# Last 128 rows of w1 on 64 partitions, and a reshaped tail, in a decode step of attention and SwiGLU

## Chip, cores, metric

One core of one Trainium2 chip. Time is device microseconds (us) of one execution; medians of several executions are quoted. Runs 1 to 4 were on one chip, runs 5 to 11 on another.

## The reference, cut to what matters

```python
x = A_x                                  # [4, 1, 640], bf16
xn = layernorm(x)
# attention: 32 heads of 192, the last 2048 positions of the cache (8192 long), wq [640, 6144], wo [6144, 640]
# SwiGLU: h = silu(xn @ w1) * (xn @ w3);  h @ w2,  w1 and w3 [640, 1536], w2 [1536, 640]
return x + attention(xn, k_cache, v_cache, wq, wo) + swiglu(xn, w1, w3, w2)
```

Four tokens read 223 MB of cache and weights (222.97 MB on q1 in the page of the kernel before). Nothing is used twice, so the DMA is the work.

## The kernel before

All loads are issued on one queue (SyncE). K and V of a head are 3 MB each, one row of 24,576 bytes per partition. w1 and w3 are loaded in one transfer each, five rows of 3,072 bytes per partition. The queue ends with the last two V, the first eight chunks of w2, two pieces of wo, and two pieces of w2 of two chunks each.

```python
def load_v(h):
    vt = vpool.tile([P, NJ, Dh], BF16, tag="vt")
    nc.sync.dma_start(out=vt[:].rearrange("q j d -> q (j d)"),
                      in_=v_win[:, h].rearrange("b (p j) d -> p b (j d)", p=PB))
    vts[h] = vt
# ... cut ...
def ffn_load(name, w):
    wt = fpool.tile([P, KC, F], BF16, tag="w", name=name)          # P = 128, KC = 5, F = 1536
    nc.sync.dma_start(out=wt[:].rearrange("p k n -> p (k n)"), in_=w.rearrange("(p kc) n -> p (kc n)", kc=KC))
    ffn[name] = wt

def ffn_in(name):                                                   # xn @ w1 or xn @ w3
    ffn["ps"] = ps_t.tile([P, FW], FP32, tag="t", name="f_ps")
    for kc in range(KC):
        for w in range(HG):
            nc.tensor.matmul(ffn["ps"][w * CT:(w + 1) * CT, :], lhsT=xnT[:, kc].rearrange("p a b -> p (a b)")[:, 0:CT],
                             rhs=ffn[name][:, kc, w * FW:(w + 1) * FW], start=(kc == 0), stop=(kc == KC - 1))
# ... cut ...
W2C = [0, FC - 4, FC - 2, FC]                                       # FC = 12 chunks of w2
# ... cut: the schedule; its end loads V 30 and 31, w2 piece 0, wo 6 and 7, w2 pieces 1 and 2 ...
nc.vector.tensor_copy(out=res[:, 0:N0 // 2], in_=acc[0:NR, 0:N0 // 2])
nc.scalar.copy(out=res[:, N0 // 2:N0], in_=acc[0:NR, N0 // 2:N0])
```

## Time and profile before

| | before |
|---|---|
| time, median of 3 | 527.62 us |
| span of the profile | 525.5 us |
| DMA queue q1, share of 16 engines | 98.9% |
| PE, DVE busy | 67%, 66% |
| last landing of w2 | 521.79 us |

From the page of the kernel before: the busy tenths of the DMA in 40 slices, and the DMA queues (packets, megabytes, share of the time of 16 engines); the line of q10, 16 packets in 0.01 MB, is left out here and below.

```profile
DMA  8999999999999999999999999999999999999995
...
q1 hardware_dynamic: 11536, 222.97, 98.9%
q8 instruction: 15, 0.25, 0.2%
q14 instruction: 5, 0.04, 0.0%
```

The DMA is full nearly from start to end: 9 tenths in every slice but the first and the last. Two small queues share its engines: 15 packets of 16,384 bytes and 5 of 8,192 bytes inside the span, both of kind "instruction"; this document calls them fetches.

The chain of waits of the kernel before, from 514 us on (start, duration, what):

```profile
490.75 31.04 DMA w<-in_B_w_dram
521.79 0.04 issue
521.83 0.45 PE acc L214 x4
522.28 0.02 issue
522.31 0.33 DVE res L442
522.63 0.02 issue
522.66 0.28 ACT res L443
```

The end waits for the last w2 piece; then come four matmuls and two copies, one after the other (both read and write the same tiles; `--waits` has the second, on ACT, released by the first, on DVE), and the output.

In the traces a load over 128 partitions raises its semaphore (the counter that others wait for) 16 times, and at most 16 data packets are under way at once (overlaps of a few ns aside). The packets have no engine numbers; each of the 16 times is read here as the landing on one engine. Here are those of the last w2 piece, sorted (us):

```
518.55 518.61 518.71 518.81 518.96 519.29 519.48 520.00 | 521.44 521.47 521.58 521.60 521.64 521.69 521.69 521.79
```

Eight engines are done about 2 us before the other eight, though all carry the same bytes of q1. The packet records tell why. A data packet of 24,576 bytes takes 912 ns, and an engine starts the next one 908 ns after the last, all the way. Where a q8 packet falls on an engine, it takes 0.88 to 0.96 us itself and the data packet after it takes 1.37 to 1.46 us in place of 0.91: about 1.4 us lost on that engine. A q14 packet takes 0.31 us itself; the data packet after it took 1.44 us in three cases of five, so about 0.85 us was lost, and 1.15 and 1.19 us in the other two.

The q8 packets, all of 16,384 bytes, come one every 26 to 39 us. By the end, engines with equal bytes of q1 are up to 3.2 us apart (518.55 and 521.79 us).

### The profile page before, as it was taken

What the parts mean: (1) busy time and instruction counts of PE and PEld (TensorE: products, weight loads), DVE (VectorE), ACT (ScalarE), POOL (GpSimd) and SP (SyncE); (2) the same over time, 40 slices, a digit from 0 to 9 for tenths busy, and PEclk for the clock granted to TensorE, in tenths of its full rate; (3) what the DMA queues carried; (4) which work ended last, traced back from release to release, by engine and by line L of the source; (5) the groups of instructions that cost most, each with busy time, mean ns of one, the idle gap of its engine ahead of it and who ended that gap; (6) DMA issues with size and microseconds to landing.
All of it is one profiled execution on the core that took longest, in us unless ns stands there. A gap on an engine that the chain in (4) does not pass through costs nothing.

```text
span 525.5 us, 4734 instructions
## 1 busy us (share of the span) xinstructions
PE 354.6 (67%) x2307; PEld 74.0 (14%) x1613; DVE 345.2 (66%) x435; ACT 45.9 (9%) x144; POOL 1.1 (0%) x8
## 2 busy tenths in 40 slices
PE   2765766567747687667748866686685776675685
PEld 0000111111101111011111211111111111111122
DVE  3179755479557767587656776577667766677671
ACT  2111201000000001000000000000000000000001
POOL 0000000000000000000000000000000000000000
PEclk9989978979889979798887998789878998889988
DMA  8999999999999999999999999999999999999995
GB/s 360 430 438 425 440 431 424 436 428 439 425 433 431 435 426 432 434 427 439 430 427 440 425 434 430 436 428 435 432 428 434 430 430 436 430 434 430 434 422 240
DMA packets 11572, 223.26 MB, mean 425 GB/s; under 512 B 1296, under 2 KB 1312, under 8 KB 2592
## 3 DMA queue, kind: packets, MB, share of 16 engines
q1 hardware_dynamic: 11536, 222.97, 98.9%
q8 instruction: 15, 0.25, 0.2%
q14 instruction: 5, 0.04, 0.0%
q10 hardware_dynamic: 16, 0.01, 0.0%
HBM read 222.96 MB, written 0.01 MB: 424 GB/s over the span
## 4 chain that ended last, share of the span: by engine, by line
DMA 66%; PE 17%; DVE 14%; ACT 2%; issue 1%; SPq 0%
DMA kt<-in_A_k_cache_dram 52%; PE ps L244 10%; DVE pr L233 10%; DMA w<-in_B_w_dram 6%; DMA vt<-in_A_v_cache_dram 5%; PE po L317 4%; DMA wt<-in_A_wq_dram 4%; DVE sc L252 2%; PE qps L193 1%; ACT ex L280 1%; DVE z L288 1%; PE mt L274 1%; PE mt L261 0%; ACT negm L277 0%; DVE qbc L199 0%
## 5 line engine op out<-in xcount | busy, mean ns | idle before, releaser
L244 PE MATMUL ps<-pr,idb 128*128 128x512 bf16 x768 | 211.5, 417 | 151.0 <-DVE pr L233 151.0
L233 DVE TENSOR_TENSOR pr<-kt,qbc 128x3072 bf16<-128x3072 bf16 x128 | 223.5, 1747 | 113.8 <-DMA kt<-in_A_k_cache_dram 113.8
L252 DVE TENSOR_REDUCE sc<-ps 128x16 f32<-128x512 f32 x128 | 87.2, 681 | 2.1 <-PE ps L244 2.1
L296 PE MATMUL o_ps<-vt,z 128*8 128x384 bf16 x1024 | 57.4, 365 | 0.2 <-DVE z L288 0.2
L317 PE MATMUL po<-o_sb,sel_w 128*32 128x192 f32 x128 | 49.2, 518 | 0.6 <-ACT o_sb L299 0.6
L296 PEld LDWEIGHTS <-z 128*8 128x8 bf16 x1024 | 25.5, 92 | 91.7 <-issue 81.2
L299 ACT COPY o_sb<-o_ps 128x384 f32<-128x384 f32 x32 | 15.3, 478 | 190.1 <-PE o_ps L296 190.1
L288 DVE TENSOR_TENSOR z<-ex,mask_b 128x256 bf16<-128x256 bf16 x32 | 13.6, 424 | 23.4 <-ACT ex L280 23.4
L277 ACT COPY negm<-mt 128x1 f32<-128x1 f32 x32 | 5.1, 159 | 256.1 <-PE mt L274 256.1
L261 PEld LDWEIGHTS mt<-idf,lmax 128*1 128x1 f32 x32 | 3.2, 100 | 140.8 <-issue 140.8
L193 PE MATMUL qps<-wt,xnT 128*128 128x512 bf16 x60 | 16.1, 428 | 5.1 <-DMA wt<-in_A_wq_dram 5.1
L317 PEld LDWEIGHTS po<-o_sb,sel_w 128*32 128x32 f32 x128 | 13.8, 130 | 29.7 <-issue 28.2
L244 PEld LDWEIGHTS <-idb 128*128 128x128 bf16 x124 | 11.9, 96 | 39.1 <-issue 32.6
L274 PEld LDWEIGHTS mt<-ones_ff,gneg 1*128 1x128 f32 x64 | 9.4, 183 | 46.3 <-issue 20.9
L199 DVE CAST qbc<-qps 128x512 bf16<-128x512 f32 x6 | 3.8, 685 | 18.0 <-PE qps L193 18.0
L274 PE MATMUL mt<-ones_ff,gneg 1*128 1x1 f32 x64 | 12.1, 256 | 0.6 <-DVE gneg L269 0.6
L266 DVE TENSOR_REDUCE gmax<-mt 1x4 f32<-1x128 f32 x32 | 8.8, 274 | 5.4 <-PE mt L261 5.4
L304 PEld LDWEIGHTS po<-rsum,tot_w 128*32 128x32 f32 x64 | 4.4, 108 | 55.6 <-issue 30.6
L280 ACT ACTIVATE ex<-sc,negm 128x64 bf16<-128x64 f32 x32 | 11.1, 348 | 1.0
L261 PE MATMUL mt<-idf,lmax 128*1 128x128 f32 x32 | 11.0, 344 | 0.0
L214 PE MATMUL acc<-wo_t,oT 128*4 128x320 bf16 x96 | 9.2, 298 | 0.6 <-DMA wo_t<-in_A_wo_dram 0.6
L304 PE MATMUL po<-rsum,tot_w 128*32 128x1 f32 x64 | 7.1, 181 | 1.3 <-ACT ex L280 1.3
(53 smaller groups left out, 62.7 us busy)
## 6 DMA issues: line engine op xcount, KB each, us to landing
kt<-in_A_k_cache_dram SPq DMA_DIRECT2D x32, 3072.0 KB, 18.8
vt<-in_A_v_cache_dram SPq DMA_DIRECT2D x32, 3072.0 KB, 25.9
wo_t<-in_A_wo_dram SPq DMA_DIRECT2D x8, 960.0 KB, 21.5
wt<-in_A_wq_dram SPq DMA_DIRECT2D x2, 3072.0 KB, 9.8
w<-in_B_w_dram SPq DMA_DIRECT2D x2, 1920.0 KB, 21.5
wt<-in_A_wq_dram SPq DMA_DIRECT2D x1, 1536.0 KB
w<-in_B_w_dram SPq DMA_DIRECT2D x1, 1280.0 KB, 32.8
w<-in_B_w_dram SPq DMA_DIRECT2D x2, 320.0 KB, 31.0
```

What stands on the lines that cost most here:

```text
L193: nc.tensor.matmul(qp[:], lhsT=xnT[:, kc].rearrange("p a b -> p (a b)"), rhs=wq_rows[kc][:, (c0 + i) * QC:(c0 + i + 1) * QC], start=(kc == ...
L233: nc.vector.tensor_tensor(out=pr[:], in0=kts[h][:, g * JQ:(g + 1) * JQ, :], in1=qbc[:, h * Dh:(h + 1) * Dh].unsqueeze(1).to_broadcast([P, ...
L244: nc.tensor.matmul(ps[:], lhsT=idb[:], rhs=pr[:, :, kk * DD:(kk + 1) * DD], start=(kk == 0), stop=(kk == NK - 1))
L252: nc.vector.tensor_reduce(out=scs[h][:, g * JQ:(g + 1) * JQ], in_=pss.pop(u)[:], axis=AX.X, op=ALU.add)
L261: nc.tensor.transpose(out=mt[0:1, 0:P], in_=chs[h][0][:], identity=idf[:])
L274: nc.tensor.matmul(mt[:, P:P + 1], lhsT=gneg[:].rearrange("o p b -> o (p b)"), rhs=ones_ff[0:1, 0:1], start=True, stop=True)
L280: nc.scalar.activation(out=ex[:], in_=scs.pop(h)[:], func=ACTF.Exp, bias=negm[:, 0:1], scale=SCALE, accum_out=rsum[:])
L288: nc.vector.tensor_tensor(out=z[:], in0=ex[:].unsqueeze(2).to_broadcast([P, NJ, B]), in1=mask_b[:].unsqueeze(1).to_broadcast([P, NJ, B]), ...
L296: nc.tensor.matmul(o_ps[c * CT:c * CT + 2 * B, :], lhsT=z[:, 2 * jj:2 * jj + 2, :], rhs=vt[:, 2 * jj:2 * jj + 2, :], start=(jj < 4), stop= ...
L299: nc.scalar.copy(out=o_sb[:], in_=o_ps[:])
L304: nc.tensor.matmul(po[sl, Dh:Dh + 1], lhsT=tot_w[:].rearrange("p a b -> p (a b)"), rhs=rsums.pop(h)[:], start=True, stop=True)
L317: nc.tensor.matmul(po[sl, 0:Dh], lhsT=sel_w[:, par].rearrange("p a b -> p (a b)"), rhs=o_sb[:, par * Dh:(par + 1) * Dh].rearrange("p (r i) ...
```

## The change

The intent, as it can be read: take load off late engines by loading the last fifth of w1 in two transfers that eight engines carry and that fill partitions 0-63, and shorten the tail: a last w2 piece of one chunk, one copy of the result. w3, w2 and the last V are cut into more transfers. The room comes from the second copy of x and a smaller tile of ones. The core of the diff:

```diff
-    def load_v(h):
+    def load_v(h, n=1):
         vt = vpool.tile([P, NJ, Dh], BF16, tag="vt")
-        nc.sync.dma_start(...)
+        for j in range(0, NJ, NJ // n):
+            nc.sync.dma_start(out=vt[:, j:j + NJ // n]..., in_=...)
@@ cut: x_load and its tile x_res go, x_add uses x_sb; ones_ff [P, P] -> [1, 1] @@
+    LP = P // 2
+    LE, LI = 8, 4
+    LX = (KC - 1) * P
@@ cut: ffn_x, which transposes xn for the new order of rows @@
     def ffn_load(name, w):                       # now for w3 alone
-        nc.sync.dma_start(out=wt[:].rearrange("p k n -> p (k n)"), in_=w.rearrange("(p kc) n -> p (kc n)", kc=KC))
+        for k0, k1 in ((0, KC // 2), (KC // 2, KC)):
+            nc.sync.dma_start(out=wt[:, k0:k1, :]..., in_=...)
+    def ffn_load_low(name, w):
+        wt = fpool.tile([P, KC + 1, F], BF16, tag="w", name=name)
+        nc.sync.dma_start(out=wt[:, 0:KC - 1, :].rearrange("p k n -> p (k n)"),
+                          in_=w[0:LX, :].rearrange("(p kc) n -> p (kc n)", kc=KC - 1))
+        for g in range(2):
+            rows_g = w[LX + g * LP:LX + (g + 1) * LP, :]
+            nc.sync.dma_start(out=wt[g * CT:(g + 1) * CT, KC - 1:KC + 1, :].rearrange("p k n -> p (k n)"),
+                              in_=rows_g.rearrange("(i e j) n -> e i (j n)", i=LI, e=LE))
@@ cut: ffn_in takes a list of (lhsT, partitions); ffn_in_low uses four chunks of 128 rows and two of 64 @@
-    W2C = [0, FC - 4, FC - 2, FC]
+    W2C = [0, FC - 8, FC - 4, FC - 1, FC]
-    add(3, 0, ffn_load, "w1", B_w1)
-    add(11, 7, ffn_in, "w1")
+    add(3, 0, ffn_load_low, "w1", B_w1)
+    add(6, 7, ffn_x)
+    add(11, 7, ffn_in_low, "w1")
@@ cut: the end now loads V 30, V 31 in two halves, w2 pieces 0 and 1, wo 6 and 7, w2 pieces 2 and 3 @@
-    nc.vector.tensor_copy(out=res[:, 0:N0 // 2], in_=acc[0:NR, 0:N0 // 2])
-    nc.scalar.copy(out=res[:, N0 // 2:N0], in_=acc[0:NR, N0 // 2:N0])
+    nc.vector.tensor_copy(out=res[:], in_=acc[0:NR, :])
```

The order `e i` with e = 8 in the source of the small transfers is deliberate.

More of the change, by code (lines that the diff above doesn't have):

```diff
@@ L111, in load_k @@
         kts[h] = kt
-    def load_v(h):
+    def load_v(h, n=1):
         vt = vpool.tile([P, NJ, Dh], BF16, tag="vt")
-        nc.sync.dma_start(out=vt[:].rearrange("q j d -> q (j d)"),
-                          in_=v_win[:, h].rearrange("b (p j) d -> p b (j d)", p=PB))
+        for j in range(0, NJ, NJ // n):
+            nc.sync.dma_start(out=vt[:, j:j + NJ // n].rearrange("q j d -> q (j d)"),
+                              in_=v_win[:, h].rearrange("b (p j) d -> p b j d", p=PB)[:, :, j:j + NJ // n].rearrange("p b j d -> p b (j d)"))
         vts[h] = vt
@@ L140 @@
     make_identity(nc, idf[:])
-    ones_ff = const.tile([P, P], FP32, name="ones_ff")
+    ones_ff = const.tile([1, 1], FP32, name="ones_ff")
     nc.vector.memset(ones_ff[:], 1.0)
@@ L220 @@
     po = ps_po.tile([P, Dh + 1], FP32, name="po")
-    xr = {}
-    def x_load():
-        xr["t"] = const.tile([B, D], BF16, name="x_res")
-        nc.sync.dma_start(out=xr["t"][:], in_=A_x.rearrange("b s d -> (b s) d"))
     def x_add(i):
-        acc_half(i, idb[0:B, 0:B], xr["t"], first=True)
+        acc_half(i, idb[0:B, 0:B], x_sb, first=True)
     def mult(u):
@@ L273, in chain_bc @@
         lmax, mt, gneg = chs[h]
-        nc.tensor.matmul(mt[:, P:P + 1], lhsT=gneg[:].rearrange("o p b -> o (p b)"), rhs=ones_ff[0:1, 0:1],
+        nc.tensor.matmul(mt[:, P:P + 1], lhsT=gneg[:].rearrange("o p b -> o (p b)"), rhs=ones_ff[:],
                          start=True, stop=True)
@@ L338, with ffn_x @@
     ffn = {}
+    LP = P // 2
+    LE, LI = 8, 4
+    LX = (KC - 1) * P
+    xn_l = const.tile([B, 2, LP], BF16, name="xn_l")
+    xnF = const.tile([P, KC + 1, NREP, B], BF16, name="xnF")
+    def ffn_x():
+        for j in range(2):
+            nc.vector.tensor_copy(out=xn_l[:, j].rearrange("b (g e i) -> b g e i", e=LE, i=LI),
+                                  in_=xn[:, LX:D].rearrange("b (g i e j) -> b j g e i", i=LI, e=LE, j=2)[:, j])
+        ps = ps_t.tile([P, KC + 1, B], BF16, tag="t", name="xnF_ps")
+        for kc in range(KC - 1):
+            nc.tensor.transpose(out=ps[:, kc, :], in_=xn[:, kc:LX:KC - 1], identity=idb[0:B, 0:B])
+        for j in range(2):
+            nc.tensor.transpose(out=ps[0:LP, KC - 1 + j, :], in_=xn_l[:, j, :], identity=idb[0:B, 0:B])
+        nc.vector.tensor_copy(out=xnF[:, 0:KC - 1], in_=ps[:, 0:KC - 1, :].unsqueeze(2).to_broadcast([P, KC - 1, NREP, B]))
+        nc.vector.tensor_copy(out=xnF[0:LP, KC - 1:KC + 1],
+                              in_=ps[0:LP, KC - 1:KC + 1, :].unsqueeze(2).to_broadcast([LP, 2, NREP, B]))
@@ L340, in ffn_load @@
     def ffn_load(name, w):
-        wt = fpool.tile([P, KC, F], BF16, tag="w", name=name)
-        nc.sync.dma_start(out=wt[:].rearrange("p k n -> p (k n)"), in_=w.rearrange("(p kc) n -> p (kc n)", kc=KC))
+        wt = fpool.tile([P, KC + 1, F], BF16, tag="w", name=name)
+        for k0, k1 in ((0, KC // 2), (KC // 2, KC)):
+            nc.sync.dma_start(out=wt[:, k0:k1, :].rearrange("p k n -> p (k n)"),
+                              in_=w.rearrange("(p kc) n -> p kc n", kc=KC)[:, k0:k1, :].rearrange("p k n -> p (k n)"))
@@ L343, in ffn_load @@
         ffn[name] = wt
-    def ffn_in(name):
+    def ffn_load_low(name, w):
+        wt = fpool.tile([P, KC + 1, F], BF16, tag="w", name=name)
+        nc.sync.dma_start(out=wt[:, 0:KC - 1, :].rearrange("p k n -> p (k n)"),
[4 more added lines that the diff above has]
+                              in_=rows_g.rearrange("(i e j) n -> e i (j n)", i=LI, e=LE))
+        ffn[name] = wt
@@ L346, in ffn_in @@
+    def ffn_in(name, parts):
         ffn["ps"] = ps_t.tile([P, FW], FP32, tag="t", name="f_ps")
-        for kc in range(KC):
+        for k, (lhsT, np_) in enumerate(parts):
             for w in range(HG):
-                nc.tensor.matmul(ffn["ps"][w * CT:(w + 1) * CT, :], lhsT=xnT[:, kc].rearrange("p a b -> p (a b)")[:, 0:CT],
-                                 rhs=ffn[name][:, kc, w * FW:(w + 1) * FW], start=(kc == 0), stop=(kc == KC - 1))
+                nc.tensor.matmul(ffn["ps"][w * CT:(w + 1) * CT, :], lhsT=lhsT,
+                                 rhs=ffn[name][0:np_, k, w * FW:(w + 1) * FW], start=(k == 0), stop=(k == len(parts) - 1))
@@ L352, in ffn_silu, with ffn_in_all, ffn_in_low @@
+    def ffn_in_all(name):
+        ffn_in(name, [(xnT[:, kc].rearrange("p a b -> p (a b)")[:, 0:CT], P) for kc in range(KC)])
+    def ffn_in_low(name):
+        ffn_in(name, [(xnF[0:n, k].rearrange("p a b -> p (a b)"), n)
+                      for k, n in [(kc, P) for kc in range(KC - 1)] + [(KC - 1, LP), (KC, LP)]])
     def ffn_silu():
@@ L411 @@
         add(a + 1, 6, ge_proj, hg, RPP // 2, RPP)
-    add(3, 0, ffn_load, "w1", B_w1)
-    add(11, 7, ffn_in, "w1")
+    add(3, 0, ffn_load_low, "w1", B_w1)
+    add(6, 7, ffn_x)
+    add(11, 7, ffn_in_low, "w1")
     add(11, 9, ffn_silu)
     add(15, 0, ffn_load, "w3", B_w3)
-    add(23, 7, ffn_in, "w3")
+    add(23, 7, ffn_in_all, "w3")
     add(23, 9, ffn_h)
-    add(8, 0, x_load)
     add(16, 6, x_add, 0)
@@ L423 @@
     for h in range(H - 2, H):
-        add(NU - 6, 0, load_v, h)
+        add(NU - 6, 0, load_v, h, h - H + 3)
     add(NU - 6, 0, w2_load, 0)
+    add(NU - 6, 0, w2_load, 1)
     add(NU - 6, 0, wo_load, NG - 2)
     add(NU - 6, 0, wo_load, NG - 1)
-    add(NU - 6, 0, w2_load, 1)
     add(NU - 6, 0, w2_load, 2)
+    add(NU - 6, 0, w2_load, 3)
     add(e - 1, 8, ffn_out, 0)
+    add(e - 1, 8, ffn_out, 1)
     add(e - 1, 8, ge_proj, NG - 2, 0, RPP)
     add(e, 6, ge_proj, NG - 1, 0, RPP)
-    add(e, 7, ffn_out, 1)
     add(e, 7, ffn_out, 2)
+    add(e, 7, ffn_out, 3)
     for s in sorted(sched):
```

## The prediction

> **What bounds the kernel now.** The DMA engines. The page's slices show DMA at 9 tenths from the second to the last but one; queue q1 fills 98.9% of the 16 engines' span; PE and DVE are busy 67% and 66%; the chain of waits is 66% DMA and ends with 31 us of a w2 load. In the trace's packet records each engine runs its packets back to back (24,576 B every 908 ns, 7,680 B every 287 ns: 0.0368 ns per byte plus 4 ns per packet), and no engine runs dry before the end. So the time is that of the most loaded engine.
>
> The engines do not finish together. The semaphore of the last w2 piece rises eight times at 518.55 to 520.00 us and eight times at 521.44 to 521.79 us. All carry the same bytes of q1; what differs is 15 packets of 16,384 B on q8 ("instruction"), falling in rotation on eight engines, each costing about 1.4 us; some 8 KB packets on q14 (about 0.85 us) fall on others. The kernel waits for the late eight.
>
> **What the change does.** The last 128 rows of w1 (24,576 B per engine) go through two transfers onto partitions 0-63.[...]
>
> - Late eight: 24,576 B less, -0.90 us; the splits of w3, last V and w2 add 24 packets x 4 ns and three semaphore writes x 6 ns, +0.11. Net -0.79: last landing 521.0 us.
> - Early eight: +0.90, +0.05 for packets and semaphores, +0.11. Net about +1.07: last landing 521.07 us.
>
> The engines become level; the DMA ends 0.7 us sooner, not more, since the mean load is unchanged.
>
> - Tail: after the last landing now 4 matmuls (0.45 us), DVE copy 0.32 us, then ACT copy 0.28 us, one after the other, then out. After: 2 matmuls, partly delayed by the 6 of the piece before: saves 0.1 to 0.25 us. One DVE copy of 320 columns, estimated at 0.49 us from 160 columns in 0.32 and 512 in 0.69, saves about 0.15 us.
> - x_res (5 KB) is on early engines and off the path. The added casts, transposes and matmuls hide in idle time of DVE and PE. Splitting w3 and V shortens no wait.
>
> **Predicted.** 527.62 - 0.7 - 0.2 - 0.15 = 526.55 us; range 525.9 to 527.2. Faster by over 2%: 0.01; within 2%: 0.98; slower by over 2%: 0.01.
>
> **What would show it.** The 16 landings of the last w2 piece lie within about 1.5 us without the gap of 1.4 us, the last near 521.0; the w1 pieces are 64 packets of 6,144 B on eight engines; the span is about 524.5; DVE's res copy takes about 0.5 us, with no ACT copy.
>
> **What would make it wrong.** If the eight engines of the small transfers are the late ones, the time rises by about 1 us. If q8 fetches move to other engines, or one more falls before the end, about 1 us is lost. If a transfer costs its engines more than 6 ns, the gain shrinks.

The sum came to 526.55 us (the terms as written give 526.57). That the late eight get the -0.79 us and the early eight the +1.07 us, and so the term of -0.7, was the assumption. The 4 ns per packet and 6 ns per semaphore write are differences of the packet spacings (908 ns for 24,576 bytes and 287 ns for 7,680; 7.27 us for eight packets and the write). In the trace before, x_res has three landings at 71.67 to 71.81 us and one at 72.92, and is first read at 85.9 us.

## The result, and the profile after

| | before | after |
|---|---|---|
| time, median (6 runs each) | 527.57 us | 527.76 us |
| span of the profile | 525.5 us | 525.9 us |
| last landing of w2 | 521.79 us | 522.46 us |
| from there to the end of the span | 3.7 us | 3.4 us |

The ratio is 1.0003, with a 95% interval of 0.9990 to 1.0016. (A ratio is the mean time of one kernel's runs over that of the other's of the same rounds, so not quite the ratio of the medians quoted.) That is the same within 2%, as foreseen, but the gain of 1.07 us is not there, and 527.76 lies outside the range of 525.9 to 527.2.

The queues of the changed kernel:

```profile
q1 hardware_dynamic: 12040, 222.96, 98.9%
q8 instruction: 15, 0.25, 0.2%
q14 instruction: 5, 0.04, 0.0%
```

504 packets more for the same bytes; the fetches are as many as before. The 16 landings of the last w2 piece after the change, in an ordinary list from the trace:

```
518.12 518.12 | 519.46 519.65 519.78 520.30 520.38 | 520.78 520.85 520.88 520.90 520.94 521.03 521.13 | 522.33 522.46
```

Fourteen engines are where the prediction had all sixteen, below 521.2 us. Two are 1.2 us behind, and two are earlier than any was before. The levelling worked on most engines, and the kernel waits for the two on which it did the opposite.

The chain of waits of the changed kernel, from 514 us on:

```profile
515.08 2.76 PE o_ps L291 x32
517.84 0.02 issue
517.86 0.49 ACT o_sb L294
...
519.90 3.16 PE acc L215 x36
523.06 0.02 issue
523.08 0.48 DVE res L477
```

In this execution no DMA ends the chain: work on the last head reached PE late and kept it busy past the last landing. Two windows of the same stretches say why it was so near (duration, then busy time and instructions of PE, PEld, DVE, ACT, POOL, then granted clock, DMA share, GB/s); first before, then after:

```profile
515.00:518.50 3.50, 2.92 (x42) 1.43 (x32) 0.00 (x0) 0.48 (x1) 0.00 (x0) 0.57 0.98 402
518.50:522.50 4.00, 2.85 (x39) 1.42 (x34) 0.99 (x3) 0.00 (x0) 0.00 (x0) 1.00 0.38 154
```

```profile
515.00:518.50 3.50, 2.84 (x35) 1.04 (x38) 0.10 (x2) 0.48 (x1) 0.00 (x0) 0.50 0.98 410
518.50:522.50 4.00, 4.00 (x48) 2.44 (x46) 0.80 (x2) 0.00 (x0) 0.00 (x0) 0.70 0.41 165
```

The clock granted to PE in the second stretch was 0.70 after and 1.00 before, and its matmuls into acc took up to 474 ns each until 520.8 us, in place of 296 to 300 (as they did again from 521 us on). The last K had also landed later, at 498.47 in place of 498.00 us, for the same late engine. But the end of DMA alone would have held the kernel nearly as long: the repeat of the changed kernel below ends at 525.8 us with the DMA at the end of its chain. There the granted clock was 1.00 in both stretches, and the span was only 0.06 us shorter (525.82 for 525.87), so the slow clock is not what was lost. The late engines are the cause to be tested.

**Which engines.** The trace has no engine numbers, but after the change the engines label themselves: eight have taken the low rows of w1 and eight have not. The first K after w1 lands at 53.90 to 54.14 us on eight engines and at 55.48 to 56.73 us on the other eight. Each q8 fetch that hits one of the first group moves it out of it. Here are the landings of the group not given low rows, at chosen transfers, with the first landing after the gap:

```
after the fetch at   landings of the early group                       next
(none)               53.90 53.96 53.99 54.02 54.05 54.11 54.12 54.14   55.48   8 engines
 57 us               61.16 61.27 61.28 61.31 61.36 61.39 61.41         62.68   7
 88 us               92.53 92.61 92.66 92.73 92.74 92.77               94.03   6
121 us               126.35 126.41 126.45 126.47 126.51                127.72  5
151 us               157.74 157.78 157.83 157.86                       159.05  4
183 us               186.88 186.93 186.94                              188.11  3
221 us               225.54 225.56                                     226.81  2
(end, last w2)       518.12 518.12                                     519.46  2
```

Six of the engines without low rows are hit by q8, and two of them never are. So q8 does not fetch on exactly the eight without low rows: some fetches go to engines that have the low rows. One of these shows at the end: the latest four landings of the last V half are 511.70, 511.85, 513.08 and 513.45 us, after 508.09, 508.20 and 509.38 us for the half before, which is 3.65 us earlier for an undisturbed engine. The newcomer at 513.45 follows the fetch at 511.4 us. The other late engine is the last from the start: it leaves its group at 56.73 us after a q14 fetch at 54.5, and again after q14 fetches at 208 and 360 us. It was never touched by a q8 packet that the landings show; three q14 fetches (the data packets after them took 1.44 us each) made it as late as two of q8.

The lengths of the q8 packets add something (ns, in order of time):

```
changed kernel   941 936 921 961 968 951 879 881 | 941 933 922 960 960 955 885
run 9, the same  938 924 960 960 954 879 879 936 | 931 924 966 961 947 879 886
before           936 921 964 960 947 881 886 934 | 929 921 962 961 947 879 879
```

The second half of each row repeats the first: q8 goes over eight engines in turn. In the changed kernel its seventh and eighth fetch left the early group as it was, so they fell on engines with low rows; in run 9, the same kernel, it was the sixth and seventh (the group goes 7, 6, 5, 4, 3, 3, 3, 2). The turn had begun one engine later, and with 15 fetches both of these engines were hit twice there, but only one of them in the changed kernel's profile. By its lengths the kernel before began as run 9 did, so its late eight were five engines outside the low-row eight and three inside (two by q8, one by q14). The trace of the kernel before alone can't show this. Where the turn begins thus differs between executions of one kernel; what sets it stays open.

### The profile page after: what moved, and what is told of

Its sections match the earlier page's. It is cut to its first block, busy times and chain, and to the rows that moved or that the text cites. A ratio compares the mean times of both kernels' runs of the same rounds, so it can differ in the third digit from the quotient of the medians.

```text
span 525.9 us, 4762 instructions
## 1 busy us (share of the span) xinstructions
PE 352.9 (67%) x2316; PEld 74.2 (14%) x1623; DVE 345.7 (66%) x439; ACT 45.6 (9%) x143; POOL 1.1 (0%) x8
## 4 chain that ended last, share of the span: by engine, by line
DMA 60%; DVE 23%; PE 14%; ACT 2%; issue 1%; SPq 0%
DMA kt<-in_A_k_cache_dram 56%; DVE pr L228 15%; PE ps L239 7%; DMA wt<-in_A_wq_dram 4%; DVE sc L247 4%; PE po L312 3%; PE qps L194 1%; DVE z L283 1%; ACT ex L275 1%; PE mt L269 1%; PE acc L215 1%; PE o_ps L291 1%; ACT L275 0%; DVE oT L320 0%; DVE og L317 0%
## 5 line engine op out<-in xcount | busy, mean ns | idle before, releaser
L291 PE MATMUL o_ps<-vt,z 128*8 128x384 bf16 x1024 | 55.9, 357 | 0.2 <-DVE z L283 0.2
L312 PE MATMUL po<-o_sb,sel_w 128*32 128x192 f32 x128 | 49.1, 517 | 0.6 <-ACT o_sb L294 0.6
L291 PEld LDWEIGHTS <-z 128*8 128x8 bf16 x1024 | 25.1, 91 | 86.5 <-issue 75.4
L312 PEld LDWEIGHTS po<-o_sb,sel_w 128*32 128x32 f32 x128 | 13.7, 129 | 29.4 <-issue 27.9
L269 PEld LDWEIGHTS mt<-ones_ff,gneg 1*128 1x128 f32 x64 | 9.4, 182 | 45.0 <-issue 25.5
L269 PE MATMUL mt<-ones_ff,gneg 1*128 1x1 f32 x64 | 12.1, 256 | 0.6 <-DVE gneg L264 0.6
```

Of the source, the lines that this page charges most:

```text
L269: nc.tensor.matmul(mt[:, P:P + 1], lhsT=gneg[:].rearrange("o p b -> o (p b)"), rhs=ones_ff[:], start=True, stop=True)
L291: nc.tensor.matmul(o_ps[c * CT:c * CT + 2 * B, :], lhsT=z[:, 2 * jj:2 * jj + 2, :], rhs=vt[:, 2 * jj:2 * jj + 2, :], start=(jj < 4), stop= ...
L312: nc.tensor.matmul(po[sl, 0:Dh], lhsT=sel_w[:, par].rearrange("p a b -> p (a b)"), rhs=o_sb[:, par * Dh:(par + 1) * Dh].rearrange("p (r i) ...
```

## Experiments

Theory A: of the engines that fetches make late, most are outside the eight that get low rows but two are inside (three, where the turn begins as in run 9); the change lifts those inside by about 1 us, and they end the kernel. Rival B: the added transfers and packets cost what was gained. Rival C: engines go with partitions, or the lower 64 partitions are slow themselves. Rival D: the compute chain holds the end.

### 1. The change without its w1 part

```diff
-    add(3, 0, ffn_load_low, "w1", B_w1)
-    add(6, 7, ffn_x)
-    add(11, 7, ffn_in_low, "w1")
+    add(3, 0, ffn_load_one, "w1", B_w1)      # one transfer, as before
+    add(11, 7, ffn_in_all, "w1")
```

> The change without its w1 part: w1 in one transfer over all 16 engines again, the rest as in the changed kernel. Theory A (the added w1 bytes sit on eight engines of which two are also hit twice by q8 fetches, and these two end last): the gap returns to eight early and eight late landings of the last w2 piece, the last at 521.9 us, and the shorter tail is kept: 527.4 to 527.5 us, about 0.3 us under the changed kernel. Rival B (the extra transfers and packets of the splits cost what was lost): last landing still near 522.4, 527.7 to 527.8 us.

Measured: 527.33 us, beside 527.72 us of the kernel before on that chip (ratio 0.9993, interval 0.9981 to 1.0006). The eight-and-eight pattern is back:

```
518.65 518.78 518.85 518.86 519.20 519.32 519.56 520.38 | 521.43 521.79 521.82 521.87 521.89 521.93 521.95 522.09
```

The chain of waits of this run:

```profile
498.23 23.45 DMA w<-in_B_w_dram
521.68 0.04 issue
521.72 0.72 PE acc L215 x8
522.45 0.02 issue
522.47 0.48 DVE res L481
```

The tail's gain stays, so the loss is in the w1 part. The time was a little under the expected 527.4 to 527.5 us, and the last landing was 522.09, not 521.9. The chain names the landing of the piece before the last, at 521.68 us: its six matmuls and the last two take 0.72 us together, longer than the last chunk needs to follow. A last piece of one chunk therefore saves less than two matmuls' time.

### 2. The w1 part alone

The low load and the residual from x_sb on the kernel before; w3, V, w2 and the two copies of the result as before.

> The w1 part alone (with the residual from the first copy of x, which frees the room for it) on the kernel before: w3, last V, w2 and the result copy as before. Theory A: two landings of the last w2 piece at 522.6 to 522.8 us, some 1.3 us after the other fourteen; 528.3 to 528.6 us. Rival B: without the splits the levelling works, 526.7 to 527.2 us.

Measured: 528.20 us beside 527.72 us (ratio 1.0008, interval 0.9995 to 1.0020). Landings: fourteen from 517.80 to 521.30 us, then 522.33 and 522.34. The chain:

```profile
491.30 31.04 DMA w<-in_B_w_dram
522.34 0.04 issue
522.38 0.45 PE acc L215 x4
522.83 0.02 issue
522.86 0.33 DVE res L480
```

The last landing is 0.55 us later than before, with w3, V and w2 loaded as before (only w1 itself goes in three transfers): rival B falls as the cause. The medians are 0.48 us apart, though the interval of the ratio still includes 1. The expectation was 0.1 to 0.4 us too high: it added the full 0.95 us to the latest of the late eight, while the two engines inside, by subtraction, were among the first of them (522.34 - 0.90 is 521.44 us, the first of the late eight before).

### 3. The same 64 partitions, outermost dimension 16

```diff
-    LE, LI = 8, 4           # two transfers of 32 partitions
+    LG, LE, LI = 1, 16, 4   # one transfer of 64 partitions
```

> The changed kernel, but the last 128 rows of w1 go onto the same 64 partitions in one transfer whose slowest dimension is 16, not 8. If the count of engines follows that dimension (theory A), all 16 carry the same bytes: landings as in the kernel before, last at 521.9, 527.4 to 527.5 us. Rival C (engines belong to partitions, so 64 partitions mean eight engines, or the lower 64 partitions are themselves the cost): as the changed kernel, two landings near 522.4, 527.7 to 527.8 us.

Measured: 528.23 us beside 527.72 us (ratio 1.0013, interval 0.9999 to 1.0027). The pattern of landings is as theory A has it (eight from 519.44 to 521.13 us, eight from 522.35 to 522.83), but all of it is about 0.9 us late, which neither theory had foreseen. So the count of engines follows the outermost dimension, not the partitions: on the same 64 partitions, 16 outside leave the eight-and-eight pattern, while the transfers with 8 outside show nine increments in the changed kernel's trace, one at once (28.09 and 28.88 us) and eight on landing (47.21 to 47.55 and 48.17 to 48.47 us).

The 0.9 us belong to the other half of rival C. The 64 low packets of 6,144 bytes took 234 ns each in the changed kernel; here 23 of them took over 300 and up to 475 ns, the later ones, and eight K packets right after them over 1.4 us in place of 0.91. The DMA share and rate from 48 to 50 us (last two columns, the rest as above), first the changed kernel, then this one:

```profile
48.00:50.00 2.00, 0.00 (x0) 0.00 (x0) 0.91 (x4) 1.44 (x3) 0.00 (x0) 0.97 1.14 492
```

```profile
48.00:50.00 2.00, 0.00 (x0) 0.00 (x0) 0.91 (x3) 1.61 (x3) 0.00 (x0) 1.00 0.79 332
```

(In windows this short the share can exceed 1; compare the two with each other only.) With eight engines on these partitions none of the 64 packets was slowed (all took 234 ns); with sixteen, 23 took up to twice as long. What they had to share, no run shows.

### 4. Outermost dimension 4

```diff
-    LE, LI = 8, 4
+    LG, LE, LI = 2, 4, 8
```

> The changed kernel with slowest dimension 4 in the two small w1 transfers. Theory A: four engines carry 98 KB each of these rows instead of 49 on eight, 2.7 us more than in the kernel before, twelve 0.8 us less; the two engines hit twice are among the first four[...], so two landings near 524.4 us and two near 521.5, 529.5 to 530.5 us. If the two hit engines are not among the first four, the last landing is near 521.7 and the time is 527.3 to 527.6 us. Rival C: as the changed kernel, 527.7 to 527.8 us.

Measured: 532.34 us beside 527.72 us (ratio 1.0088), beyond every expectation. The small transfers lasted until 53.54 us in place of 48.5, 52 of their 64 packets took over 300 ns, and 42 of 63 K packets near them took over 1.4 us, up to 2.04, in place of 0.91. Four engines now write 8 partitions of each small transfer each; why that slows packets of other transfers too, no run shows. One thing is clean: after it the first K lands on twelve engines by 57.50 us, and on four at 60.48, 60.49, 60.58 and 61.55. The last is the engine that q14 had just hit, and it stays last to the end (527.17 us). So the engine with three q14 fetches is one of the four that carry these transfers ("the first four" of the expectation; no run shows numbers). It is the only one so late (the next lands at 524.98 us), so the engine that q8 hits twice is not among these four, as the expectation had it.

### 5. Double dose

```diff
-    add(15, 0, ffn_load, "w3", B_w3)
-    add(23, 7, ffn_in_all, "w3")
+    add(15, 0, ffn_load_low, "w3", B_w3)
+    add(23, 7, ffn_in_low, "w3")
```

> Double dose: the last 128 rows of w3 go the way of those of w1. Theory A (two late engines are among the eight that take these rows): the two late landings of the last w2 piece come another 0.9 us later, near 523.4 us, two early ones near 517.3; 528.5 to 528.9 us. Rival D (the changed kernel is held by its compute chain after the last K, not by the two engines): 527.8 to 528.1 us, because compute gets no longer.

Measured: 528.81 us beside 527.51 us (ratio 1.0023, interval 1.0011 to 1.0036). The last two landings are 523.35 and 523.36 us, 1.1 us after the rest; the first is at 516.90. The chain:

```profile
499.50 23.45 DMA w<-in_B_w_dram
522.96 0.04 issue
523.00 0.73 PE acc L215 x8
523.73 0.02 issue
523.75 0.48 DVE res L477
```

With the dose at none (run 1), one and two, the last landing goes 522.09, 522.46, 523.36. By the packet lengths the turn of q8 began at the same engine in these three. The step from one to two is the 0.90 us of the bytes. The first step is smaller because without low rows the latest engines are others. Rival D falls: compute got no longer, and the end came a microsecond later.

### 6. The tail alone

As run 1, with w3 and V in one transfer each as well.

> Only the tail of the change: one result copy, last w2 piece one chunk, w2 in four pieces, residual from the first x; w1, w3 and V in one transfer each. Last landing of w2 at 521.8 to 521.9 us, eight early and eight late; 527.2 to 527.35 us, at or a little under the run with w1 whole but w3 and V split[...].

Measured: 527.54 us beside 527.51 us (ratio 1.0000, interval 0.9988 to 1.0013), last landing 521.96 us. That is a miss: it was to be at or under run 1, and it is 0.2 us over it, on another chip. The cost of the splits can't be read from these two.

### 7. Fewer PE instructions

A test of what the fetches are. Four tiles (the partial sums of O, their selector, the softmax shift and its one) in bf16, on the changed kernel; results still agree with the reference.

```diff
-    sel_w = const.tile([P, 2, NREP, B], FP32, name="sel_w")
+    sel_w = const.tile([P, 2, NREP, B], BF16, name="sel_w")
@@ the same for o_sb, gneg and ones_ff @@
```

> The changed kernel with the per-head partial sums of O, their selector and the shift of the softmax in bf16, so that 64 float32 matmuls and 32 more need one pass, not two: 192 PE instructions fewer. Theory A: q8 fetches follow PE's instructions, so the fifteenth (511 us) falls away and the others come later; of the two late engines one, hit by q8 at 250 and 511 us, joins the others near 521.0, the other, hit three times by q14, stays near 522.4 us. Time 527.4 to 527.7 us, as the one engine still holds the end while the compute chain is shorter. If fetches have nothing to do with it, two landings stay near 522.4.

The 192 are read from the changed kernel's trace: its 64 float32 matmuls of the partial sums (L312) stand there as 128, its 32 of the shift (L269) as 64, each with as many weight loads; a bf16 matmul stands once (L291: 1,024 for 1,024). Half of the doubled ones, 96 matmuls and 96 loads, were to fall away.

Measured: 528.73 us (527.73 to 529.17), beside 527.51. q8 had 14 packets, the last at 505 us, and the ones after the third came later than before, as expected if they follow PE's instructions. The rest of the expectation failed: two engines are late as before, at 522.34 and 522.50 us. The landings show a newcomer among the latest right after the fetch at 505 us, and the third engine of the untouched group is now hit at 296 us, by the eighth fetch, not at 221 by the sixth. So the turn of q8 began one engine later than in the changed kernel's profile, as it did in run 9 without any change of the kernel; that kept the engine twice hit which was to be spared. The shift is therefore no sign of the fewer instructions. The time is odd as well: over five executions it rose from 527.73 to 529.17 us while the span stayed at 525.7 to 526.1, so that the growth lies outside the span. It stays unexplained.

### 8. The tail alone, with fewer PE instructions

> The tail alone and the bf16 of the run before together. The six engines that q8 hits twice still end last, near 521.8 us, so the DMA gains nothing; after it the end waits for 8 matmuls at most: 527.1 to 527.3 us.

Measured: 527.38 us (527.15 to 527.71), just over the expectation, beside 527.51 us (ratio 0.9998, interval 0.9985 to 1.0010). There were 14 fetches; the landings are nine early (to 520.46) and seven late (521.60 to 521.85), where run 6 had eight and eight. One fetch fewer, one late engine fewer, and no gain, since the remaining late ones set the end.

### 9, 10, 11. The changed kernel, run 1 and run 6 again, on one chip

> The changed kernel once more, on one chip with the two runs below, since the differences are as small as those between chips. Theory A: two landings of the last w2 piece near 522.4 us; span 525.8 to 526.0 us, 0.1 to 0.3 us over the kernel before of the same chip.

> The change without its w1 part, again: last landing near 522.0 us, span 525.3 to 525.5 us, 0.4 us under the changed kernel beside it.

> The tail alone, again: last landing near 521.9 us, span 525.3 to 525.5 us, as the run beside it within 0.15 us, 0.4 us under the changed kernel. If instead it equals the changed kernel, the w1 part does not explain the loss.

| | time, median of 5 | range | last landing |
|---|---|---|---|
| before, 9 runs | 527.52 | 527.35 to 527.87 | |
| 9 changed | 527.76 | 527.72 to 527.79 | 522.62 (three late, from 522.33) |
| 10 w1 whole | 527.41 | 527.24 to 527.48 | 521.99 |
| 11 tail alone | 527.44 | 527.25 to 528.10 | 522.14 |

Run 9 has three late engines where two were expected: the turn of q8 began one engine later, as told above. Run 11 has a span of 525.6 us where 525.3 to 525.5 was expected. The chain of the changed kernel here ends with the DMA:

```profile
498.70 23.54 DMA w<-in_B_w_dram
522.24 0.04 issue
522.28 0.73 PE acc L215 x8
```

On one chip every execution of the changed kernel (527.72 or more) is slower than every one with w1 whole (527.48 or less), by 0.35 us in the medians. Neither of the versions without the w1 part is proved faster than the kernel before: their intervals against it include 1. Run 11 has one execution at 528.10. No version that surely beats both was found.

## Why the prediction was wrong, point by point

- **"The DMA engines bound the kernel; the time is that of the most loaded engine": right.** Putting more bytes on engines that were already late moved the end by what the bytes take (run 5: 0.90 us), or by less where other engines had been the latest (run 2: 0.55 us).
- **"The w1 pieces are 64 packets of 6,144 B on eight engines": right.** Two semaphores show eight landings each. The late engines outside went down and the early ones inside went up about as costed: fourteen engines ended by 521.13 us.
- **The step that took the late eight to lie outside the eight of the small transfers, since the x_res packets were on engines that q8 had not hit: it failed.** The x_res packets passed at 71 us, when one of fifteen q8 fetches had fallen. That says nothing of the other fourteen. q8 goes over six engines outside the eight with low rows and two inside, so with 15 fetches one or two of those inside are hit twice; one more inside was made late by three q14 fetches, which the text put down as falling "on others" without asking which of the others, or how often. In the changed kernel's profile that makes two late engines inside, in run 9 three. The semaphore of x_res itself had a hint: three landings from 71.67 to 71.81 us and one at 72.92: one of its four engines was late already.
- **The size of that step: the term "-0.7 us" of the DMA's end was +0.67 us in the profile.** The costing of +1.07 us for engines inside was about right (0.90 us for one more dose in run 5), but it was to apply to early ones only. The prediction named this case among what would make it wrong, for all eight; it came for two, and two are enough.
- **The tail, "0.2 + 0.15 us": right in size.** From the last landing to the end of the span it is 3.72 us before, 3.41 after, 3.31 in run 1 and 3.20 in run 9; the single copy took 0.48 us.
- **"Splitting w3 and V shortens no wait": right,** as far as runs 1 and 6, and 10 and 11, show no gain from it. Its cost is too small to be read.

So the sum is: +0.67 us at the end of the DMA, -0.31 us after it, +0.36 us of span in the profiled pair; 0.2 us in the medians. Whether a smaller share of rows would have helped was not run. An estimate from the landings before says it would hardly: the late eight lay within 0.35 us (521.44 to 521.79), so that more than a little on those inside becomes the new end.

## What to carry to other kernels

Where one queue keeps all DMA engines full, look at the 16 landing times of the last transfer, not at the mean share: spare time on half of the engines may be seen there. Before shifting bytes between engines, find out for each late engine which side of the shift it is on, over the whole run; one late engine on the receiving side takes the whole gain. The number of engines followed the outermost dimension of a transfer: eight landings with 8 outside, the eight-and-eight pattern of a load on all sixteen with 16 (run 3), four engines 3 us behind twelve with 4 (run 4). Which engines these are no run shows by number. But one more dose with 8 outside made the two late engines later again (run 5: last landing 523.36 us in place of 522.46), and the engine with three q14 fetches was in the eight and in the four. If a smaller outermost dimension always takes the same engines, which is an assumption, a late engine among them can't be spared in this way. Since the turn of the fetches began at different engines in executions of one kernel, one profile doesn't settle which engines are late.

A fetch is not hidden where the DMA is full: each q8 packet cost one engine about 1.4 us (0.9 us its own, 0.5 us in the data packet after it), 15 times in 525 us. And the number of engines that write to few partitions can cost time of its own: the packets of 6,144 bytes took 234 ns with 8 engines on 64 partitions, 23 of 64 took 300 to 475 ns with 16 engines (run 3), and with 4 engines (run 4) packets of other transfers slowed too (from 912 ns to over 1.4 us in 42 of 63).
